# Row sums and gate totals added across partitions through memory instead of by mask matmuls

## The chip, the cores and the metric

The kernel runs on one core of one Trainium2 chip. The metric is the device time of one launch in microseconds (us). The core has these engines: PE (matrix products, with PEld for its weight loads), DVE, ACT and POOL (elementwise work on 128 partitions), and SP, whose instruction stream issues nearly all DMAs. Every engine works through its own stream in order; streams wait for each other by semaphores.

## The reference

q, k and v are [8 batches, 8 heads, 1152 tokens, 64] in float32. Queries are averaged in neighbouring pairs (576 left), then plain softmax attention per head:

```python
scores = scale * np.matmul(q_pool, k.transpose(0, 1, 3, 2))
attn = np.exp(scores - max); attn = attn / (np.sum(attn, axis=-1, keepdims=True) + 1e-09)
out = np.matmul(attn, v)
```

The heads are put side by side to x of [8, 576, 512]. Then, per batch, a mixture of depths: the score of a token is x times w_gate; the 128 tokens with the highest scores go through relu(xe @ w1) @ w2 (512 to 1024 to 512), and that, times sigmoid(score), is added to their rows of x; all other rows stay.

## The kernel before, in words

The unit of work is a **pair** of heads (32 pairs: 8 batches x 4), and each pair is done in two **halves** of 288 queries. A half goes through these steps, which `run` (L1210) issues for neighbouring halves in turn, so that all engine streams are fixed in the program's order:

- `scores` (L799): for each of 9 chunks of 128 keys, PE computes transposed scores (keys on partitions, queries of both heads along the row; four 64x64 tiles, L810), and ACT takes the exponential out of PSUM into p (L817). The maximum is not subtracted; a count at the end of the kernel falls back to another kernel if a sum was out of bounds.
- `folded` (L842): the sums over keys. POOL adds chunks to acc (L849, three instructions), DVE reduces p and acc through 32x32 transposes (L854) and adds the pieces (L863). What is left in the tile sum is, for each of four groups of 32 partitions, a partial sum: query i of a block stands on partition i of every group, and the four groups are still to be added.
- `weighted` (L819): PE multiplies p by v (L828), ACT copies the result out (L836), POOL adds its two parts (L838); `drained` turns it on DVE (L876), `multiplied` takes it times w_gate on POOL (L886).
- `normalized` (L893), once per pair: a matmul with the constant matrix merge (1 where two partitions have the same place in their group) adds the four groups and spreads the total to all partitions (L897); ACT adds 1e-9 and writes it into the tile sums (L907, two instructions); DVE takes the reciprocal rec (L914); POOL multiplies (x, L916). `stored` (L924) writes x to memory in the next second half.
- `gated` (L933): DVE reduces the products (L939) and multiplies by rec (L941): part, the share of this pair in the gate scores.
- `prepare_pair` (L719): POOL adds neighbouring queries (qp, L725), DVE turns keys and queries (kT, qT, L728 and L732) for the next pair, in the first half of a pair (the even one).

After a batch's fourth pair, `routed` (L957) is started. It is a generator, and `units` (L1204) advances it by one unit at the end of each half: out<-xs copies the batch (L964), line is the sum of part over pairs (L968); then a matmul with merge (L977) and an ACT copy (L981) make total, which goes to memory (L984) and comes back as a row on all partitions (L985) and as columns (L986, L987); two units of comparisons on DVE (L1031, L1040, L1050) and a third with the last comparisons and five picks (L1073: for each token tile, which of the 128 slots it takes); a unit with a matmul of the picks (L1083) and a gather by POOL (L1095); later the transposes (L1109), the first expert layer (L1120, 64 matmuls), and the second (L1133, 16 matmuls) with the scatter. So a batch's routing stretches over the halves of the next batches, and what stands next to what in PE's stream is set by the number of units.

`load_pair` (L697) issues on SP the loads of k, q and v of the pair after the next, at the start of a pair's second half. kb and qb have two buffers, v_sb three, and p two. A weight load follows in each of the first halves. The order on SP in a second half is: k, q, v of pair n + 2, the stores of x of pair n - 1, a weight piece.

## Time and profile before

| what | value |
|---|---|
| median of 3 runs (lowest to highest) | 734.17 us (733.55 to 735.32) |
| the profiled execution | 734.3 us |
| its span, first to last instruction | 732.6 us |
| DMA packets | 387,857, of them 375,648 under 512 B |
| L897, the mask matmul of a pair | 64 instructions, 290 ns each |
| L907, its two evictions on ACT | 64 instructions, 272 ns each |
| L914, the reciprocal | 32, 224 ns |
| DMAs k, q, v / x stores | 124 each of 144 KB / 128 of 72 KB |

A line of a group reads: line of the kernel, engine, operation, output<-input, shape and count, then busy us and mean ns of one, then idle time of the engine just before them and who ended it. A line of the timeline reads: start in us, duration in us, engine (SPq for DMAs issued by SP), line, operation, tiles, count, and in brackets the idle time before it and its releaser. A line of waits reads: who waited for whom, us in total, times, longest. Matmuls overlap their neighbours, so starts tell more than durations.

### The profile page before, as it was taken

To read this page: it belongs to the slowest core of one execution; us is meant where nothing else is said; L and a number is where in the kernel's file an instruction comes from. 1 tells how busy PE (TensorE), PEld (TensorE's weight loads), DVE (VectorE), ACT (ScalarE), POOL (GpSimd) and SP (SyncE) were. 2 spreads that over 40 slices of the span, in tenths; PEclk is the share of its full clock that TensorE was granted. 3 is DMA by queue.
4 is the path that set the end of the run, shared out by engine and by line. 5 is a ranking of instruction groups with operands and counts; after the bars stand their busy time and mean duration, and the time that the engine had idled before them with its cause. 6 is when DMAs were issued, how large, how long until landed. Compare 5 with 4: busy or idle time off the path is not lost. (4 is left out here: it accounts for less than half of the span.)

```text
span 732.6 us, 23508 instructions
## 1 busy us (share of the span) xinstructions
PE 719.4 (98%) x10096; PEld 493.4 (67%) x10096; DVE 519.6 (71%) x758; ACT 400.9 (55%) x772; POOL 480.6 (66%) x459
## 2 busy tenths in 40 slices
PE   8999999999999999999999999999999999999996
PEld 6678886768567685766757676576756768567663
DVE  3876668976499754997649885497856978479540
ACT  5666666564466634666446654666436664466320
POOL 5787777774676866757757666676657766577620
PEclk9999999999999999999999999999999999999998
DMA  8998897995487726967278562985628965351230
GB/s 164 175 180 168 171 194 131 144 150 130 85 146 129 129 82 107 152 101 130 82 140 141 98 110 87 156 138 106 100 87 156 145 106 110 78 103 18 37 103 22
DMA packets 387857, 87.67 MB, mean 120 GB/s; under 512 B 375648, under 2 KB 375648, under 8 KB 387488
## 3 DMA queue, kind: packets, MB, share of 16 engines
q1 hardware_dynamic: 386240, 81.30, 62.7%
q0 software_dynamic: 1280, 4.20, 2.0%
q8 instruction: 81, 1.33, 0.8%
q10 hardware_dynamic: 224, 0.59, 0.3%
q14 instruction: 32, 0.26, 0.1%
HBM read 74.50 MB, written 20.99 MB: 130 GB/s over the span
## 5 line engine op out<-in xcount | busy, mean ns | idle before, releaser
L817 ACT ACTIVATE p<-ps 128x576 f32<-128x576 f32 x576 | 319.5, 689 | 5.2 <-issue 3.5
L810 PE MATMUL ps<-qT,kT 64*64 64x288 f32 x4608 | 295.7, 406 | 0.5 <-DVE qT L794 0.5
L849 POOL TENSOR_TENSOR acc<-p 128x576 f32<-128x576 f32 x192 | 267.1, 1420 | 44.2 <-ACT p L817 42.4
L828 PE MATMUL ps<-p,v_sb 64*64 64x288 f32 x4608 | 293.9, 403 | 0.0
L828 PEld LDWEIGHTS ps<-p,v_sb 64*64 64x64 f32 x4608 | 204.1, 133 | 77.9 <-ACT p L817 15.2
L810 PEld LDWEIGHTS ps<-qT,kT 64*64 64x64 f32 x4608 | 177.6, 132 | 101.0 <-ACT p L817 27.3
L854 DVE TRANSPOSE_TENSOR_REDUCE fold<-p 128x54 f32<-128x1728 f32 x64 | 126.0, 1969 | 109.7 <-ACT p L817 109.7
L854 DVE TRANSPOSE_TENSOR_REDUCE fold<-acc 128x54 f32<-128x1728 f32 x64 | 124.9, 1951 | 57.0 <-POOL acc L849 57.0
L836 ACT COPY two<-ps 128x576 f32<-128x576 f32 x64 | 40.9, 640 | 206.4 <-PE ps L828 199.7
L916 POOL TENSOR_TENSOR x<-avb,rec 128x576 f32<-128x576 f32 x32 | 37.1, 1159 | 116.5 <-DVE rec L914 112.4
L838 POOL TENSOR_TENSOR av<-two 128x288 f32<-128x288 f32 x64 | 51.1, 798 | 18.4 <-ACT two L836 14.6
L1120 PEld LDWEIGHTS ps<-xeT,w 128*128 128x128 f32 x512 | 58.0, 192 | 3.7 <-issue 2.6
L1120 PE MATMUL ps<-xeT,w 128*128 128x128 f32 x512 | 59.7, 277 | 0.7 <-ACT xeT L1112 0.7
L1133 PE MATMUL ps<-w,hT 128*128 128x512 f32 x128 | 57.0, 597 | 0.0
L886 POOL TENSOR_TENSOR prod<-avb,w_gate 128x288 f32<-128x288 f32 x64 | 51.0, 797 | 1.9 <-DVE avb L876 1.9
L725 POOL TENSOR_TENSOR qp<-qb 128x576 f32<-128x576 f32 x31 | 43.5, 1403 | 7.3 <-DMA qb<-in_q_dram 7.3
L728 DVE STREAM_TRANSPOSE kT<-kb 128x1152 f32<-128x1152 f32 x31 | 42.4, 1369 | 0.3 <-issue 0.3
L1133 PEld LDWEIGHTS ps<-w,hT 128*128 128x128 f32 x128 | 23.6, 190 | 26.3 <-issue 26.3
L941 DVE TENSOR_TENSOR part<-red,rec 128x18 f32<-128x18 f32 x32 | 39.7, 1239 | 1.1
L1128 ACT ACTIVATE hT<-ps 128x512 f32<-128x512 f32 x16 | 9.6, 598 | 48.6 <-PE ps L1120 48.6
L1073 DVE TENSOR_SCALAR pick<-slot_f,rank 128x128 f32<-128x128 f32 (+1 forms) x40 | 32.8, 883 | 0.4
L876 DVE STREAM_TRANSPOSE avb<-av 128x288 f32<-128x288 f32 x64 | 29.1, 455 | 5.3 <-POOL av L838 5.2
(81 smaller groups left out, 313.2 us busy)
## 6 DMA issues: line engine op xcount, KB each, us to landing
kb<-in_k_dram SPq DMA_DIRECT2D x124, 144.0 KB, 4.3
qb<-in_q_dram SPq DMA_DIRECT2D x124, 144.0 KB, 4.6
v_sb<-in_v_dram SPq DMA_DIRECT2D x124, 144.0 KB, 4.0
xs<-x SPq DMA_DIRECT2D x128, 72.0 KB, 3.4
out_dram<-xs SPq DMA_DIRECT2D x8, 1152.0 KB, 5.8
w<-in_moe_w_dram SPq DMA_DIRECT2D x8, 512.0 KB, 5.0
sc_row<-row SPq DMA_DIRECT2D x7, 288.0 KB, 3.2
acc<-in_q_dram ACTq DMA_DIRECT2D x2, 288.0 KB, 5.3
```

Source lines behind the costliest of these rows:

```text
L725: nc.gpsimd.tensor_tensor(out=qp[:, :, :], in0=pair["q"][:, :, 0, :], in1=pair["q"][:, :, 1, :], op=ALU.add)
L728: nc.vector.transpose(kT.rearrange("p (c g i) -> p c g i", c=self.NC, i=BLK), pair["k"].rearrange("p (g c) d -> p c g d", c=self.NC),)
L810: nc.tensor.matmul(sc[keys, j, 0:n], lhsT=pair["kT"][rows, c * P + keys.start : c * P + keys.stop], rhs=pair["qT"][rows, qs], start=True, ...
L817: nc.scalar.activation(p[:, c // G, c % G, :, :], sc[:, :, 0:n], AF.Exp, scale=self.scale)
L828: nc.tensor.matmul(av[j * self.D : (j + 1) * self.D, e, 0:n], lhsT=half["pair"]["v"][keys, j, c, :], rhs=half["p"][keys, c // G, c % G, j, :],
L836: nc.scalar.copy(two[:, :, :], av[:, :, 0:n])
L838: nc.gpsimd.tensor_tensor(out=half["av"][:, :], in0=two[:, 0, :], in1=two[:, 1, :], op=ALU.add)
L849: nc.gpsimd.tensor_tensor(out=acc[:, u, :], in0=units[:, 0, u, :], in1=units[:, 1, u, :], op=ALU.add)
L854: nc.vector.tensor_reduce(fold[:, a, :], of.rearrange("p u (m d) -> p (u m) d", d=BLK), AX.X, ALU.add, apply_transpose=True,)
L886: self.nc.gpsimd.tensor_tensor(out=pair["prod"][:, ns, :], in0=pair["avb"][:, ns, :], in1=self.w_gate[:, hp : hp + 1, :].broadcast_to([P, ...
L1120: nc.tensor.matmul(pv[:, f, 0:w], lhsT=self.w1[:, c, (f0 + f) * P : (f0 + f + 1) * P], rhs=xeT[:, c, 0:w], start=(c == 0), stop=(c == self ...
L1133: nc.tensor.matmul(ps[0:w, 0 : self.Dm], lhsT=hT[:, f, 0:w], rhs=self.w2[:, f, :], start=(f == 0), stop=(f == self.NFC - 1),)
```

## The change

The row sums of a pair are no longer merged by a matmul. `sums_out` writes the tile sum (whose layout is now by head, then block) to memory, and `sums_back` reads it with four DMAs so that each lane gets the four partial sums of its query side by side in the tile five; a fifth place holds the constant 1e-9, and one DVE reduce adds the five. The last pair keeps the matmul and its two evictions. The totals of the gate go the same way for batches 0 to 5: part is written, read as 16 numbers per query, and reduced on DVE; the write and the read each have a unit of their own, so that `routed` yields once more there. Batches 6 and 7 keep the old way. `load_pair` is split: the loads of v (`load_values`) stand on SP between the write and the read of the sums.

```diff
--- before.py
+++ after.py
@@ -645,8 +645,12 @@
         nc.vector.tensor_copy(
             self.merge[:, :, :], self.same[:, :].unsqueeze(1).broadcast_to([P, P // BLK, BLK])
         )
-        self.tiny = const.tile([P, 1], F32, name="tiny")
-        nc.gpsimd.memset(self.tiny[:, :], 1e-9)
+
+        self.five = []
+        for i in range(2):
+            five = const.tile([P, 5, self.QB], F32, name=f"five{i}")
+            nc.gpsimd.memset(five[:, 4, :], 1e-9)
+            self.five.append(five)
     def tokens(self):
         nc = self.nc
@@ -696,25 +700,29 @@
     def load_pair(self, b, hp):
-
         nc = self.nc
         kb = self.load.tile([P, self.KB, BLK], F32, name="kb")
         qb = self.load.tile([P, self.QB, 2, BLK], F32, name="qb")
-        v_sb = self.load.tile([P, 2, self.NC, self.D], F32, name="v_sb", bufs=3)
         for j, ds, rows in self.quarters():
             of = self.k[b, 2 * hp + j, :, ds]
             nc.sync.dma_start(kb[rows, :, :], of.rearrange("(i n) d -> i n d", i=BLK))
         for j, ds, rows in self.quarters():
             of = self.q[b, 2 * hp + j, :, ds].rearrange("(i m) d -> i m d", i=BLK)
             nc.sync.dma_start(qb[rows, :, :, :].rearrange("i n r d -> i (n r) d"), of)
-        of = self.v[b, 2 * hp : 2 * hp + 2]
+        return {"k": kb, "q": qb, "b": b, "hp": hp}
+
+    def load_values(self, pair):
+
+
+        nc, hp = self.nc, pair["hp"]
+        v_sb = pair["v"] = self.load.tile([P, 2, self.NC, self.D], F32, name="v_sb", bufs=3)
+        of = self.v[pair["b"], 2 * hp : 2 * hp + 2]
         of = of.rearrange("j (i g c) d -> g i j c d", i=BLK, c=self.NC)
         for g in range(P // BLK):
             nc.sync.dma_start(
                 v_sb[g * BLK : (g + 1) * BLK, :, :, :].rearrange("i j c d -> i j (c d)"),
                 of[g].rearrange("i j c d -> i j (c d)"),
             )
-        return {"k": kb, "q": qb, "v": v_sb, "b": b, "hp": hp}
     def prepare_pair(self, pair):
@@ -859,13 +867,32 @@
                 apply_transpose=True,
             )
         if half["s"] == 0:
-            pair["sum"] = self.small.tile([P, 2, nb], F32, name="sum")
+            pair["sum"] = self.small.tile([P, 2, self.QB], F32, name="sum")
+        ns = slice(half["s"] * self.HB, (half["s"] + 1) * self.HB)
         nc.vector.tensor_reduce(
-            pair["sum"][:, half["s"], :],
-            fold.rearrange("p a (u n) -> p n (a u)", n=nb),
+            pair["sum"][:, :, ns],
+            fold.rearrange("p a (u j n) -> p j n (a u)", j=2, n=self.HB),
             AX.X,
             ALU.add,
         )
+
+    def last_pair(self, pair):
+        return pair["b"] == self.B - 1 and pair["hp"] == self.NPAIR - 1
+
+    def sums_out(self, pair):
+
+        row = pair["row"] = self.dram.tile([P, 2, self.QB], F32, name="row_sums")
+        self.nc.sync.dma_start(row[:, :, :], pair["sum"][:, :, :])
+
+    def sums_back(self, pair):
+
+        quad = P // BLK
+        five = pair["five"] = self.five[pair["hp"] % 2]
+        for j, _, rows in self.quarters():
+            self.nc.sync.dma_start(
+                five[rows, 0:quad, :],
+                pair["row"][:, j, :].rearrange("(g i) n -> i g n", i=BLK),
+            )
     def drained(self, half):
@@ -892,23 +919,28 @@
     def normalized(self, pair):
-        nc, hb, hp = self.nc, self.HB, pair["hp"]
-        ps = self.banks()[:, 0, :]
-        nc.tensor.matmul(
-            ps[:, 0 : 4 * hb],
-            lhsT=self.merge.rearrange("p g j -> p (g j)"),
-            rhs=pair["sum"].rearrange("p s n -> p (s n)"),
-            start=True,
-            stop=True,
-        )
+        nc, hp = self.nc, pair["hp"]
         tot = self.sums[:, pair["b"] * self.NPAIR + hp, :]
-        for j in range(2):
-            rows = slice(j * self.D, (j + 1) * self.D)
-            nc.scalar.activation(
-                tot[rows, :].rearrange("p (s n) -> p s n", s=2),
-                ps[rows, 0 : 4 * hb].rearrange("p (s j n) -> p s j n", s=2, j=2)[:, :, j, :],
-                AF.Identity,
-                bias=self.tiny[rows, 0:1],
+        if self.last_pair(pair):
+            ps = self.banks()[:, 0, :]
+            nc.tensor.matmul(
+                ps[:, 0 : 2 * self.QB],
+                lhsT=self.merge.rearrange("p g j -> p (g j)"),
+                rhs=pair["sum"].rearrange("p j n -> p (j n)"),
+                start=True,
+                stop=True,
+            )
+            for j in range(2):
+                rows = slice(j * self.D, (j + 1) * self.D)
+                nc.scalar.activation(
+                    tot[rows, :],
+                    ps[rows, j * self.QB : (j + 1) * self.QB],
+                    AF.Identity,
+                    bias=self.five[0][rows, 4, 0:1],
+                )
+        else:
+            nc.vector.tensor_reduce(
+                tot, pair["five"].rearrange("p g n -> p n g"), AX.X, ALU.add
             )
         rec = pair["rec"] = self.small.tile([P, self.QB], F32, name="rec")
         nc.vector.reciprocal(rec[:, :], tot)
@@ -964,21 +996,41 @@
         nc.sync.dma_start(self.out[b], xs[:, :])
-        line = self.small.tile([P, self.QB], F32, name="line")
-        nc.vector.tensor_reduce(
-            line[:, :], part[:, :, :].rearrange("p n q -> p q n"), AX.X, ALU.add
-        )
         sc = ffn.tile([P, NT], F32, name="gate_sc")
+        if b >= self.B - 2:
+            line = self.small.tile([P, self.QB], F32, name="line")
+            nc.vector.tensor_reduce(
+                line[:, :], part[:, :, :].rearrange("p n q -> p q n"), AX.X, ALU.add
+            )
         if b < self.B - 1:
-            yield True
+            total = self.small.tile([BLK, self.QB], F32, name="total")
+            if b < self.B - 2:
+                quad = P // BLK
+                row = self.dram.tile([P, self.NPAIR * self.QB], F32, name="row_gate")
+                nc.sync.dma_start(row[:, :], part.rearrange("p a n -> p (a n)"))
+                yield True
+                parts = self.small.tile([BLK, quad * self.NPAIR, self.QB], F32, name="parts", bufs=2)
+                nc.sync.dma_start(
+                    parts.rearrange("p (g a) n -> p g (a n)", g=quad),
+                    row.rearrange("(g i) x -> i g x", i=BLK),
+                )
+                yield True
+                nc.vector.tensor_reduce(
+                    total[:, :], parts.rearrange("p a n -> p n a"), AX.X, ALU.add
+                )
+            else:
+                yield True
+                ps = self.banks()[:, 0, 0 : self.QB]
+                nc.tensor.matmul(
+                    ps,
+                    lhsT=self.merge.rearrange("p g j -> p (g j)"),
+                    rhs=line[:, :],
+                    start=True,
+                    stop=True,
+                )
+                nc.scalar.copy(total[:, :], ps[0:BLK, :])
             sc_row = ffn.tile([P, NT * P], F32, name="sc_row")
-            ps = self.banks()[:, 0, 0 : self.QB]
-            nc.tensor.matmul(
-                ps, lhsT=self.merge.rearrange("p g j -> p (g j)"), rhs=line[:, :], start=True, stop=True
-            )
-            total = self.small.tile([BLK, self.QB], F32, name="total")
-            nc.scalar.copy(total[:, :], ps[0:BLK, :])
             row = self.dram.tile([Sp], F32, name="row")
             nc.gpsimd.memset(sc[:, NF:], 0.0)
             nc.sync.dma_start(row.rearrange("(i n) -> i n", i=BLK), total[:, :])
@@ -1219,6 +1271,8 @@
         self.prepare_first(upcoming)
         self.tokens()
         loaded = self.load_pair(*pairs[1]) if len(pairs) > 1 else None
+        if loaded:
+            self.load_values(loaded)
         weights = self.weight_loads()
         for h in range(n_halves + 1):
             if h < n_halves:
@@ -1241,6 +1295,13 @@
                 if h > 2:
                     self.gated(halves[h - 3])
                 self.folded(half)
+                if s == 1:
+                    if not self.last_pair(pair):
+                        self.sums_out(pair)
+                    if loaded:
+                        self.load_values(loaded)
+                    if not self.last_pair(pair):
+                        self.sums_back(pair)
                 if h > 1:
                     self.multiplied(halves[h - 2])
                 if s == 0 and loaded:
```

## The prediction

> **What bounds the kernel now.** I read the page's busy shares first, then the waits, then PE's timeline, and last DVE and POOL where PE meets them.
>
> ```profile
> PE 719.4 (98%) x10096; PEld 493.4 (67%) x10096; DVE 519.6 (71%) x758; ACT 400.9 (55%) x772; POOL 480.6 (66%) x459
> PEclk9999999999999999999999999999999999999998
> DMA  8998897995487726967278562985628965351230
> ```
>
> PE is busy for all but 13 us of the span at a full granted clock, so whatever leaves PE's stream shortens the run, until something makes PE wait. The DMA row is high in the first ten slices.
>
> ```profile
> L897 PE MATMUL ps<-sum,merge 128*128 128x36 f32 x64 | 13.2, 290 | 0.0
> L897 PEld LDWEIGHTS ps<-sum,merge 128*128 128x128 f32 x64 | 9.5, 188 | 14.0 <-issue 14.0
> ```
>
> These are the groups that leave PE. Their busy time is not their price, since matmuls overlap; the price is the step from start to start in PE's timeline:
>
> ```profile
> 314.93 4.59 PE L828 MATMUL ps<-p,v_sb 64*64 64x288 f32 x72
> 319.46 0.41 PE L897 MATMUL ps<-sum,merge 128*128 128x36 f32 x2
> 319.70 1.34 PE L1083 MATMUL ps<-meta,pick 128*128 128x3 f32 x10
> 320.98 4.60 PE L810 MATMUL ps<-qT,kT 64*64 64x288 f32 x72
> ```
>
> Here the mask matmul takes 0.24 us (319.46 to 319.70). The same stretch on DVE and POOL:
>
> ```profile
> 315.68 4.79 DVE L1073 TENSOR_SCALAR pick<-slot_f,rank 128x128 f32<-128x128 f32 x5
> 320.39 0.43 DVE L939 TENSOR_REDUCE red<-prod 128x9 f32<-128x288 f32 x1
> ...
> 313.94 4.14 POOL L849 TENSOR_TENSOR acc<-p 128x576 f32<-128x576 f32 x3 [1.34 <-ACT p L817]
> 318.03 0.80 POOL L886 TENSOR_TENSOR prod<-avb,w_gate 128x288 f32<-128x288 f32 x1
> 318.79 1.40 POOL L725 TENSOR_TENSOR qp<-qb 128x576 f32<-128x576 f32 x1
> ...
> PE ps L1083 <- DVE pick L1073: 0.6, 2, 0.3
> ```
>
> The five picks (selection masks that PE multiplies at L1083) take 4.79 us; the smallest of all picks takes 0.27. Cut finer, the timeline shows each ending as a POOL instruction ends (316.72, 318.08, 318.83, 320.19), so beside a POOL without gaps a pick lasts one POOL instruction. The last pick ends at 320.46; PE wants it about 1.0 us after L1083 starts, at 320.7. PE hardly waits for picks now (0.6 us in the run), with 0.3 us to spare.
>
> **The change on PE.** The profiled execution took 734.3 us (span 732.6 and 1.7 around it), 0.1 above the median of the runs, 734.17. Removed:
> - 31 of 32 L897: the matmul's step is 0.24 us, 7.4 in all.
> - 6 of 7 L977: 0.22 to 0.31 us of step, 1.4 in all.
> - Switches of tiling. L828 before an L897 steps 4.50 us on average, before L810 4.38; and L897 steps 0.34 instead of 0.24 when L810 follows: 0.22 per excursion into 128-row work. The order of instructions has 39 such excursions before and 27 after (expert work, moved by half a pair, now has odd halves of its own). 12 x 0.22 = 2.6.
> - ACT loses 62 evictions of 0.272 us that stood ahead of the exponentials; scores after an L897 step 4.42 against 4.37, with one of 4.80: about 1.0.
>
> Saving 12.4 us, taken as 12. Bounds: 9 (the two steps alone) and 15 (busy time of both groups).
>
> **What it adds beside PE.** DVE gets 31 reduces of 90 elements, between L968 (72 elements, 278 ns) and L863 (108, 340 ns): 0.3 us, 9.6 in all, hidden in DVE's idle 29% except in the chain below. Six reduces of 288 elements (L939 has 416 ns) replace six L968. L863's output order costs nothing: same count, an idle DVE. Each pair writes 128 pieces of 144 B and reads 512 of 72 B. The q1 queue took 62.7% of 16 x 732.6 us for 386,240 packets, 19 ns each, so 640 take 0.76 us of the 16 engines: hidden where the DMA share is 0.61 (170 to 690 us), not where it is 0.93 (first 100 us).
>
> SP issues 5 more DMAs per pair, 0.33 us (row<-total) to 0.43 us (gate_sc<-row): 1.8 us. The write waits for DVE's sum, and behind it on SP stand the next v, the reads and the next pair's k and q. From sum to total: 0.33 issue, 2.7 for four v issues (which cover the write's 1.8 us landing), 1.6 for four reads, 3.1 landing as gate_sc<-row: 7.7 us. In the trace 11.3 to 14.5 us lie between the end of a pair's second sum and its reciprocal from pair 6 on, so DVE does not wait there; it would begin to if landings took 3.6 us more. In pairs 0 to 5 the gap is only 8.0 to 11.8.
>
> **The chain to the picks, the term that decides.** The extra write and read of batches 0 to 5 push the routing units one half back. Comparisons start now in an odd half, right after the second expert layer (L1133), and the picks end the third half; PE wants them at the end of the fourth. After the change the comparisons again start right after that layer, but the three halves are even, odd, even. An even half has more on DVE: kT and qT (1.29 + 0.66 us of step), rec, total. Against before the chain grows by 2.1 + 0.15 + two totals 0.54 = 2.8 us. PE comes sooner by two L897 with their switches: 36.07 us from the anchor (start of the first scores after L1133, 283.63) becomes 35.25.
>
> Step by step from that anchor, with the trace's durations: fold(p) 5.86 (as now), first rec 12.7, four comparison blocks to 15.3, second fold done 20.8 (POOL's acc comes behind x, 14.3 to 18.5), two blocks to 24.0, part 24.9, third fold 29.1, kT, qT, avb, total, rec 31.85, last block 33.6. POOL then runs x to 33.15, acc to 37.6, prod to 38.4, av to 39.2 without a gap: the picks end at 34.9, 36.25, 37.65, 38.4 and 39.25. PE finishes L1083 at 39.5 instead of 36.5. PE waits **3.0 us per batch**; for batches 1 to 5, 15 us. Bounds: 0 (picks of 0.27 to 0.34 us from 33.6 end at 35.2), and 5.1, if part (L941), two inputs of 18 elements, waits through three POOL instructions for a gap (24.4 to 27.0): L941 has 0.18 to 4.63 us, so both occur. I take the boundary case, as in L941's 0.90. Batch 6 keeps the old unit and gets the fifth batch's expert layer inside its chain: no wait.
>
> [...]
>
> **The first 170 us.** SP issues there without a pause (7.7 to 103 us), some 18 us per pair, as PE's pace; POOL already waits for q once batch 0 routes:
>
> ```profile
> 112.27 3.50 SPq L706 DMA_DIRECT2D kb<-in_k_dram  x4
> 115.81 4.98 SPq L709 DMA_DIRECT2D qb<-in_q_dram  x4
> ...
> 124.41 1.41 POOL L725 TENSOR_TENSOR qp<-qb 128x576 f32<-128x576 f32 x1 [1.89 <-DMA qb<-in_q_dram]
> ```
>
> With 1.8 us of issues and 0 to 2 us of waiting for the write (behind k and q in the queue), SP falls 2 to 3 us per pair behind. Batch 0's write of part then lands only behind the 1.15 MB copy of xs (5.8 us), and SP waits for it. The issue of k at 112.27 moves to about 118.7, its q lands near 131 instead of 124.4, and the keys are turned by 133; PE wants them at 132.42 - 3 = 129.4. That is 3.6 us of PE wait, and batch 0's comparisons and picks, behind late totals, wait as the others or more. Together 8 us; bounds 0 (SP finds the queue drained and its issues shorter, as kb at 3.3 instead of 5.2 us) and 18 (batch 0's scores back only near 140 us, its picks 13 us late).
>
> **Sum:** 734.3 - 12 + 15 + 8 = 745.3; with the median's 0.1 less, 745.
>
> **Rivals.**
> 1. Faster: the picks find POOL's gaps. Then 734.3 - 12 + 0 to 8 = 722 to 730. For it: the smallest pick is 0.27 us, and POOL's ends are the only brake. Against it: POOL's own order is x, three accs, prod and av with nothing to wait for. It is decided by whether the last pick ends by 36.25 from the anchor; each us beyond costs 5.
> 2. SP becomes the bound through the early pairs and batch 0: the early term is 18, the picks 15 to 20: 755 to 760. For it: no SP pause up to 103 us and 0.93 DMA share. Against it: PE's second expert stages (7 us each) later let SP catch up.
> 3. The totals come late in every pair, landings 5 us above the row: 1.4 us of DVE wait per pair on margins of 3.6, doubled where two totals stand in the chain: 5 x 2.8 = 14 more, 759. Against it: in the steady part the DMA engines are 39% idle.
> 4. The matmuls go but their time does not, since the switches stay: saving 9 instead of 12, 748; inside the main case.
>
> **How the numbers follow.** Main case 0.54 (own range 737 to 754, from 2 to 5 us per batch and 2 to 12 early); rival 1 0.27; rivals 2 and 3 0.14; the pieces cancel to within 0.2% 0.05. 0.2% (1.5 us) is about what this measurement can tell from no change. Slower is 0.54 + 0.14 = 0.68, faster 0.27, same 0.05. The range reaches into rival 1 (723) and to the upper rivals' near edge (760); under 2 in 10 is left out.
>
> **What would show it.** PE: no L897 but one, one L977; stages after odd halves without expert work step 4.37 to 4.40. Right if the waits list PE (or its loads) at L1135 on DVE pick with 2 to 5 us each, six times. Rec on DVE should follow the second sum by 11 us or more after 190 us; in the first 150 us a wait of DVE on the five tile, and one of POOL on q. SP's waits should move from POOL's x to DVE's sum. Wrong if the waits at L1135 are under 1 us: then the picks are not chained to POOL's instructions in the new place. Wrong on the early term if k and q of pair 7 land by 126 us.

## The result, and the profile after

The changed kernel takes 774.85 us (median of four runs, 772.57 to 777.25) against 734.75 us (733.55 to 735.5) for the kernel before beside it: a ratio of 1.0548, interval 1.0509 to 1.0586, so 5.5% slower. The forecast was 745 us, range 723 to 760: the sign was right, the time lies outside the range. The profiled execution took 775.86 us (span 774.1); the one before 734.3 (span 732.6). The two spans differ by 41.5 us, and that is what has to be explained.

First the page of the changed kernel: the busy shares, the granted TensorE clock and the DMA row.

```profile
PE 727.4 (94%) x10022; PEld 504.3 (65%) x10022; DVE 513.6 (66%) x789; ACT 386.1 (50%) x704; POOL 479.8 (62%) x460
PEclk9999999869999999998999989999999999999998
DMA  8777886766564566645766546666466566551130
```

PE has 74 instructions fewer, and yet 8 us more of busy time: it works more slowly in places. The clock row, which was full before, has dips: a deep one at 155 to 175 us (6 tenths of full speed) and shallow ones (8 and 9 tenths) before and behind it. PE also waits now. From the list of waits (engine, waiting line, releaser: us in all, times, longest):

```profile
PE ps L1135 <- DVE pick L1125: 25.9, 31, 8.1
DVE sums L942 <- DMA five<-row_sums: 19.8, 5, 5.3
POOL qp L733 <- DMA qb<-in_q_dram: 7.0, 3, 3.6
PE ps L818 <- DVE qT L740: 5.6, 3, 2.5
```

The first line was 0.6 us before. L1135 multiplies the picks (it was L1083), L818 is the scores (it was L810). Here is the place in batch 2 that the forecast walked through step by step, as the timeline shows it on PE, DVE and POOL (start, us, engine, line):

```profile
347.88 4.69 PE L836 MATMUL ps<-p,v_sb 64*64 64x288 f32 x72
353.19 0.35 PE L1135 MATMUL ps<-meta,pick 128*128 128x3 f32 x2 [0.62 <-DVE pick L1125]
354.46 0.38 PE L1135 MATMUL ps<-meta,pick 128*128 128x3 f32 x2 [0.91 <-DVE pick L1125]
...
357.31 0.58 PE L1135 MATMUL ps<-meta,pick 64*128 64x3 f32 x2 [0.36 <-DVE pick L1125]
357.82 7.56 PE L818 MATMUL ps<-qT,kT 64*64 64x288 f32 x72
...
351.90 5.35 DVE L1125 TENSOR_SCALAR pick<-slot_f,rank 128x128 f32<-128x128 f32 x5
...
351.57 4.10 POOL L857 TENSOR_TENSOR acc<-p 128x576 f32<-128x576 f32 x3
355.64 0.79 POOL L913 TENSOR_TENSOR prod<-avb,w_gate 128x288 f32<-128x288 f32 x1
356.39 0.79 POOL L846 TENSOR_TENSOR av<-two 128x288 f32<-128x288 f32 x1
```

The picks run from 351.90 to 357.25 beside a POOL without gaps, PE takes them one by one, and the scores after them last 7.56 us instead of 4.6. The clock in that place, from the busy time by stretch (us, then busy time and instructions of PE, PEld, DVE, ACT, POOL, then the granted clock, the DMA share and GB/s):

```profile
317.00:358.00 41.00, 37.77 (x591) 27.93 (x594) 33.90 (x61) 23.09 (x44) 30.63 (x28) 0.99 0.58 103
358.00:363.00 5.00, 5.00 (x44) 2.59 (x47) 4.60 (x6) 2.79 (x7) 1.33 (x2) 0.50 0.23 59
363.00:373.00 10.00, 10.00 (x164) 5.82 (x160) 6.68 (x8) 6.04 (x11) 6.88 (x6) 0.96 0.75 139
```

In the 5 us after the wait the granted clock is 0.50. The kernel pays twice: for the wait, and for slow matmuls after it.

I then set the 63 points at which PE begins a half's scores in both traces side by side (halves are counted from 0, and the first two begin as one). The difference (after less before) reads:

| where | difference at that point | what happened since the row above |
|---|---|---|
| first scores | -1.0 | the start is earlier; a repeat of the kernel before was 0.4 earlier too |
| half 9 (87 us) | -3.6 | four pairs without L897: 0.64 us a pair saved |
| half 21 (213 us) | +20.7 | some 27 us lost (19.0 of waits and 8 of slow work, lines below), so about 3 saved meanwhile |
| half 63 (676 us) | +41.5 | batches 1 to 5: waits 20.9 and slow scores 9.7; 9.9 saved, which is what is left over |

A half with picks lasts 14.09 to 14.31 us from scores to scores in batches 1 to 5, against 10.06 without a wait (8.78 of a half and 1.28 of the picks' matmuls in the trace before): 4.0 to 4.25 us of wait each, 20.9 in five batches. The scores' step after it is 5.82, 7.39, 6.50, 6.10 and 5.93 us against 4.41: 1.4 to 3.0 us each, 9.7 in all.

The early loss, as PE's timeline of the changed kernel shows it:

```profile
113.40 6.28 PE L818 MATMUL ps<-qT,kT 64*64 64x288 f32 x72 [2.00 <-DVE qT L740]
135.35 6.17 PE L818 MATMUL ps<-qT,kT 64*64 64x288 f32 x72 [2.53 <-DVE qT L740]
151.32 4.34 PE L818 MATMUL ps<-qT,kT 64*64 64x288 f32 x40 [3.50 <-ACT p L825]
168.17 0.56 PE L1135 MATMUL ps<-meta,pick 128*128 128x3 f32 x2 [8.09 <-DVE pick L1125]
172.80 6.22 PE L818 MATMUL ps<-qT,kT 64*64 64x288 f32 x72
```

PE waits 5.6 us for qT (1.09 of it earlier, at 93.67 us), 3.5 us for exponentials (p) and 9.9 us for batch 0's picks (8.09 and four shorter waits), 19.0 in all. The slow scores with and after these waits and the drawn-out picks make up the other 8.

### The profile page after: what moved, and what is told of

It reads as the page before. It is cut to its first block, busy times and chain, and to the rows that moved or that the text cites. A ratio compares the mean times of both kernels' runs of the same rounds, so it can differ in the third digit from the quotient of the medians.

```text
span 774.1 us, 23555 instructions
## 1 busy us (share of the span) xinstructions
PE 727.4 (94%) x10022; PEld 504.3 (65%) x10022; DVE 513.6 (66%) x789; ACT 386.1 (50%) x704; POOL 479.8 (62%) x460
## 3 DMA queue, kind: packets, MB, share of 16 engines
q8 instruction: 81, 1.33, 0.7%
## 5 line engine op out<-in xcount | busy, mean ns | idle before, releaser
L818 PE MATMUL ps<-qT,kT 64*64 64x288 f32 x4608 | 309.9, 420 | 9.8 <-DVE qT L740 5.6
L818 PEld LDWEIGHTS ps<-qT,kT 64*64 64x64 f32 x4608 | 192.8, 138 | 112.9 <-issue 23.9
L1135 PE MATMUL ps<-meta,pick 128*128 128x3 f32 (+1 forms) x80 | 16.2, 284 | 25.9 <-DVE pick L1125 25.9
L1125 DVE TENSOR_SCALAR pick<-slot_f,rank 128x128 f32<-128x128 f32 (+1 forms) x40 | 36.8, 983 | 0.4
L1135 PEld LDWEIGHTS ps<-meta,pick 128*128 128x128 f32 (+1 forms) x80 | 13.6, 220 | 32.1 <-DVE pick L1125 16.5
```

Of the source, the lines that this page charges most:

```text
L818: nc.tensor.matmul(sc[keys, j, 0:n], lhsT=pair["kT"][rows, c * P + keys.start : c * P + keys.stop], rhs=pair["qT"][rows, qs], start=True, ...
```

## The experiments

Before them stood theory A: three costs, the early transfers behind SP's queue, the picks one half later, and a lower clock after each wait of PE. Theory B: only the gate's totals cost anything, the row sums through memory are nearly free. Theory C: the traffic through memory as such.

Where a ratio is given, it is against the kernel before on the same chip. That kernel took medians of 735 to 741 us on the chips used, so differences of a few us between runs of different groups are read from the traces and not from the medians.

### The two halves of the change, and where they begin

Row sums alone (gate totals of all batches by the matmul):

```diff
-        if b >= self.B - 2:
+        if not (False):
             line = self.small.tile([P, self.QB], F32, name="line")
...
-            if b < self.B - 2:
+            if False:
                 quad = P // BLK
```

> The row sums go through memory as in the change, the gate's totals of all batches stay with the mask matmul, so nothing of the gate's routing is a half later. Theory A (three costs: the early lag of SP, the picks one half later in batches 1 to 5 at 4.2 us each, and 1.4 to 3 us each in which TensorE runs at a lower granted clock after such a wait): the five waits at L1135 are gone with what follows them (some 30 us), and part of the early loss of 28 us, so 728 to 738 us. Theory B (the row sums through memory cost nothing, the gate's totals are the whole loss): 720 to 724 us, the time before less a saving of 11 to 15 us. Theory C (the traffic through memory slows everything): above 745 us.

Measured: 744.9 us, ratio 1.012 (1.0086 to 1.0155).

The gate's totals alone (row sums of all pairs by the matmul, v loaded where it was before):

```diff
     def last_pair(self, pair):
-        return pair["b"] == self.B - 1 and pair["hp"] == self.NPAIR - 1
+        return True
...
                     loaded = self.load_pair(*pairs[n + 2]) if n + 2 < len(pairs) else None
+                    if loaded:
+                        self.load_values(loaded)
```

> The mirror image: row sums by the mask matmul and the loads of v at their old place, the gate's totals of six batches through memory with their extra half. Theory A: five waits of 4.2 us, each followed by a slow stretch of 1.4 to 3 us, and the routing of batch 0 late, without the lag of the row sums on SP: 753 to 760 us, and the mean wait of L1135 on the pick again above 4 us. Theory B: the whole loss is here, with only the gate's small part of the saving: 760 to 775 us. Theory C: six writes and 24 reads in all are little, so 740 us or less.

Measured: 763.76 us, ratio 1.0385 (1.035 to 1.042).

Both from batch 2 on:

```diff
     def last_pair(self, pair):
-        return pair["b"] == self.B - 1 and pair["hp"] == self.NPAIR - 1
+        return pair["b"] < 2 or (pair["b"] == self.B - 1 and pair["hp"] == self.NPAIR - 1)
...
-            if b < self.B - 2:
+            if 2 <= b < self.B - 2:
```

> Both routes through memory begin with batch 2; batches 0 and 1 stay with the mask matmul for row sums and gate totals. Theory A: the early loss of 28 us is gone, as are the wait and the slow stretch of batch 1 (6 us), and the saving of the eight pairs too (4 us): about 750 us. The rival, that the early loss has nothing to do with the transfers but with the order of v's loads, which is unchanged here: 765 us or more.

Measured: 748.48 us, ratio 1.0173 (1.0144 to 1.0202), as theory A had it.

Neither part is free: 9.7 us over the kernel before for the row sums, 28.6 for the gate's totals, 38.3 together, close to the 40.1 of the whole change. So B falls, and A had both too cheap (728 to 738 and 753 to 760 us). With the row sums alone the difference to before goes from -3.4 us at half 9 to +18.3 at half 16, and then falls to +10.4 at the end. That is a loss of some 22 us within seven halves and 7.9 us of gain after it. With the gate's totals alone it is +7.3 at half 17, and then it rises with each batch to +29.6. With both from batch 2 on it stays at -1.0 until half 18, falls to -5.1 by half 31, and rises from half 32 on, with batch 2's picks. C falls too: it had the gate's totals at 740 us or less, and if the traffic as such were slow, the row sums, which are most of it, would lose throughout, and they gain after half 16.

### Why the picks hold PE up

The picks in a form that also sums into a column that nobody uses:

```diff
                     scalar1=rank[0:rows, t : t + 1],
                     scalar2=None,
                     op0=ALU.is_equal,
+                    op1=ALU.add,
+                    accum_out=hits[0:rows, t : t + 1],
```

> The change as it is, but each pick (a comparison by VectorE) also sums into a column, a form that in this kernel's trace does not stand behind POOL. If the picks are late because each one lasts as long as the POOL instruction beside it (5.35 us for the run of them), they now end some 3 us or more earlier and the waits of L1135 on the pick shrink from 4.2 us to 1 us or less: about 750 us by theory A (4 to 5 us less in each of five batches, and less in batch 0). The rival, that the picks are late because their scores come back late and their own length does not matter: 770 to 775 us.

Measured: 744.87 us, ratio 1.0112 (1.0078 to 1.0145), 30 us less than the change with its own picks. The same place of batch 2 on DVE, PE and POOL:

```profile
346.65 0.34 DVE L1126 TENSOR_SCALAR_CACHE_REDUCE pick<-slot_f,rank 128x128 f32<-128x128 f32 x1
346.92 0.08 DVE L1126 DVE_READ_ACCUMULATOR pick<-slot_f,rank 128x1 f32 x1
...
347.25 1.36 PE L1138 MATMUL ps<-meta,pick 128*128 128x3 f32 x10
348.55 4.60 PE L818 MATMUL ps<-qT,kT 64*64 64x288 f32 x72
...
346.31 4.13 POOL L857 TENSOR_TENSOR acc<-p 128x576 f32<-128x576 f32 x3
```

A pick now takes 0.34 us where five took 5.35, 1.07 each on average; PE does not wait, and the scores after take 4.60. POOL is as busy as before beside it. So the start of the picks, as late as in the change (8.4 us after the start of the half's scores in both), does no harm by itself; the length of the picks beside POOL does.

The gate's write and read in one unit, with the copy of the batch's output behind them:

```diff
-        nc.sync.dma_start(self.out[b], xs[:, :])
...
                 nc.sync.dma_start(row[:, :], part.rearrange("p a n -> p (a n)"))
-                yield True
...
                 )
+                nc.sync.dma_start(self.out[b], xs[:, :])
                 yield True
```

> The change with one difference: the gate's partial sums are written and read back in one unit, ahead of the copy of the batch's output, so the extra unit is gone and the totals are added where the matmul stood before. If the loss in batches 1 to 5 comes from the extra unit (every later step of the routing one half later, so that the picks meet POOL and TensorE waits for them), the waits of L1135 on the pick shrink to 1 us or less and the time is 744 to 752 us, as with the faster picks. The rival, that the two trips through memory alone make the picks late, the unit or not: 768 to 775 us.

Measured: 748.52 us, ratio 1.0112 (1.0082 to 1.0143) on a chip where the kernel before took 740.66. In batches 1 to 4 PE does not wait for picks by more than 0.1 us, in batch 5 by 0.62 us. So the extra unit and the slow picks are both needed for the cost in batches 1 to 5: taking away either removes it. The early loss is in both runs (+20.9 us at half 21 with the accumulating picks, +17.0 with one unit).

### The lower clock after a wait

The kernel before, with seven needless reductions on DVE ahead of the picks of batches 0 to 5:

```diff
             pick = ffn.tile([P, NT, P], F32, name="pick", bufs=1)
+            if b < self.B - 2:
+                idle = ffn.tile([P, 1], F32, name="idle", bufs=1)
+                for _ in range(7):
+                    nc.vector.tensor_reduce(
+                        idle[:, :], self.slot_f[:, :], AX.X, ALU.max
+                    )
```

> The kernel before, nothing through memory; only seven needless reductions on VectorE (some 4.5 us) stand ahead of the picks of batches 0 to 5. It asks whether a wait of TensorE alone is followed by a lower granted clock. If it is: six waits of some 4 us and after each 1.4 to 3 us in slower matmuls, 33 to 42 us in all, so 766 to 777 us, with a granted clock below 0.7 in the 5 us after each wait. If the lower clock belongs to the traffic through memory: the waits alone, some 24 us, so 756 to 760 us, at a clock that stays near 1.00.

Measured: 758.6 us, ratio 1.0257 (1.0225 to 1.0288). By its time alone this would be the second answer, but the waits came out shorter than I had made them: 1.51 us in each of batches 1 to 5. The trace answers instead: first PE's timeline in batch 1, then the busy time and clock of the stretches around it:

```profile
235.66 0.41 PE L897 MATMUL ps<-sum,merge 128*128 128x36 f32 x2
237.58 1.37 PE L1089 MATMUL ps<-meta,pick 128*128 128x3 f32 x10 [1.51 <-DVE pick L1079]
238.89 6.19 PE L810 MATMUL ps<-qT,kT 64*64 64x288 f32 x72
```

```profile
230.00:235.00 5.00, 5.00 (x85) 2.92 (x84) 4.86 (x13) 2.71 (x5) 4.86 (x4) 1.00 0.96 144
235.00:240.00 5.00, 3.48 (x37) 2.40 (x32) 4.90 (x11) 1.30 (x5) 2.18 (x3) 0.87 0.84 166
240.00:245.00 5.00, 5.00 (x72) 2.80 (x68) 4.97 (x6) 4.19 (x8) 0.00 (x0) 0.78 0.01 3
```

With no partial sums going through memory, a wait of 1.5 us is followed by scores at a clock of 0.78. Their step is 6.02 to 6.11 us against 4.41, four times of five 6.10 or more: another 1.6 to 1.7 us. Of the 21.8 us by which this span is longer than before, each of batches 1 to 5 takes about 3.3, half of it wait and half clock. The lower clock belongs to the pause in PE's work, not to the trips of partial sums. How its cost goes with the pause, over the runs (idle time listed at the picks' matmul, then the scores' step, 4.41 without a pause):

| run | idle us | step us |
|---|---|---|
| row sums alone, batch 5 | 0.62 | 4.42 |
| one unit, batch 5 | 0.62 | 6.11 |
| kernel before once more, batch 0 | 1.33 | 4.42 |
| kernel before with delay, batches 1 to 5 | 1.51 | 6.02 to 6.11 |
| gate alone, batches 1 to 5 | 1.46 to 1.50 | 6.00 to 7.35 |
| the change, batches 1 to 5 | 2.83 to 3.24 | 5.82 to 7.39 |
| row sums alone, batch 0 | 8.81 | 6.82 |

The cost hardly follows the length. At 0.62 us it came once and stayed out once, at 1.33 us it stayed out, and from 1.5 us on it is 1.4 to 3.0 us whatever the length. The clock's own record shows what it goes with. In all 17 traces the granted clock is either 1.00 or 0.50, and it changes only on a grid of 3.41 us: a low stretch before the end of the kernel lasts 3.41, 6.83, 10.24 or 13.65 us, and each 3.41 us at half clock costs up to 1.7 us (half of its length, an estimate; after the waits of 1.51 us it was 1.6 to 1.7 us). Here are the two pauses of 0.62 us on that grid, first the run with one unit, then the one with the row sums alone:

```profile
598.17:601.58 3.41, 2.79 (x34) 2.08 (x34) 3.38 (x6) 1.13 (x4) 1.70 (x2) 1.00 0.64 97
601.58:604.99 3.41, 3.41 (x36) 1.93 (x32) 3.38 (x4) 2.62 (x5) 0.00 (x0) 0.50 0.84 132
```

```profile
594.49:597.90 3.41, 3.15 (x47) 1.93 (x38) 3.41 (x5) 0.64 (x1) 3.23 (x4) 1.00 0.50 117
597.90:601.31 3.41, 3.05 (x46) 2.14 (x49) 3.38 (x5) 1.71 (x5) 0.65 (x1) 1.00 0.75 116
601.31:604.72 3.41, 3.41 (x64) 2.17 (x60) 3.38 (x4) 3.41 (x7) 0.00 (x0) 1.00 0.90 142
```

In the first run the picks' matmuls and the pauses between them all fall into one window, which keeps 1.34 us of other matmuls, and the clock is 0.50 in the next; in the second they lie across a border, each window keeps 2.3 us or more, and the clock stays at 1.00. Cut into such windows, all 17 traces sort without an exception: where PE, in a window at full clock, was busy with anything but the picks' matmuls for at most 1.42 us, the clock was 0.50 in the next (56 windows); where for 1.49 us or more, it stayed at 1.00 (3528 windows). With the picks' matmuls counted as work no limit sorts them (2.80 us was followed by half clock, 1.49 us by full). So these thin matmuls, three columns each, count like pause here, and what a pause costs depends on how it lies on the grid. No run was made to move a pause along it; the sorting is read from the traces.

### The first 170 us

Row sums through memory for all pairs but the 4th, gate by the matmul:

```diff
     def last_pair(self, pair):
-        return pair["b"] == self.B - 1 and pair["hp"] == self.NPAIR - 1
+        return (pair["b"] == 0 and pair["hp"] == 3) or (
+            pair["b"] == self.B - 1 and pair["hp"] == self.NPAIR - 1
+        )
```

> Row sums through memory for every pair but the 4th, the last of batch 0; gate totals by the mask matmul, picks as they were. If the whole early loss of 22 us follows from that one pair (its sum is the last thing that batch 0's gate total waits for, and all of its routing comes after): 724 to 731 us. If the trips of pairs 5 to 8 are late on their own account: 737 to 745 us, hardly better than all pairs through memory (744.9 us).

Measured: 745.41 us, ratio 1.0079 (1.0052 to 1.0106), no better than with all pairs (744.9). With all pairs, PE stood 6.55 us ahead of batch 0's gate total (at 109.34 us) and 8.81 ahead of its picks. Here the first of these waits is gone, but PE only comes sooner to the next one, for the queries of the 8th pair:

```profile
135.48 6.07 PE L818 MATMUL ps<-qT,kT 64*64 64x288 f32 x72 [5.45 <-DVE qT L740]
141.37 4.55 PE L836 MATMUL ps<-p,v_sb 64*64 64x288 f32 x72
152.73 1.24 PE L1135 MATMUL ps<-meta,pick 128*128 128x3 f32 x4 [6.81 <-DVE pick L1125]
```

So it is not one late total; something shared is late. Two runs with row sums from batch 2 on and all gate totals by the matmul separate what. The first is without any early trip:

```diff
     def last_pair(self, pair):
-        return pair["b"] == self.B - 1 and pair["hp"] == self.NPAIR - 1
+        return pair["b"] < 2 or (pair["b"] == self.B - 1 and pair["hp"] == self.NPAIR - 1)
...
-            if b < self.B - 2:
+            if False:
```

> Row sums through memory from batch 2 on only, all gate totals by the mask matmul. In the run with all row sums through memory the kernel lost 22 us between the 9th and the 16th half and then gained 7.9 us over the rest. If the loss belongs to the first 150 us, when the DMA engines are most loaded and no expert layer lies between the halves, this run keeps the gain and about 1 us at the start: 725 to 728 us, faster than before. The rival, that the loss comes wherever the transfers begin or meets the routing of any batch: 735 us or more.

Measured: 729.64 us, ratio 0.9869 (0.9842 to 0.9895). No early loss, though v stands at its new place in SP's queue, and half a us where the trips begin. The second makes the early trips and lets nobody read what they bring:

```diff
-                    if not self.last_pair(pair):
+                    if not self.real_last(pair):
                         self.sums_out(pair)
...
-                    if not self.last_pair(pair):
+                    if not self.real_last(pair):
                         self.sums_back(pair)
```

(`last_pair`, which chooses the matmul, is true for batches 0 and 1; `real_last` for the last pair alone.)

> Row sums of batches 0 and 1 are added by the mask matmul, as in the run with row sums from batch 2 on (729.6 us), but their trips through memory are made all the same: written, waited for by SP's queue and read back into a tile that nobody reads in these pairs. If SP's queue is what made the first 170 us late: the loads of the 8th pair are issued some 8 us later, TensorE waits for its q and then for the picks, and 10 to 20 us are lost: 740 to 750 us. If the waits of VectorE and POOL for the totals are the cause, the trips alone cost next to nothing: 729 to 733 us.

Measured: 740.09 us, ratio 1.0054 (1.003 to 1.0078). In the traces the unread trips cost 10.5 us, all between halves 13 and 15: PE waits 7.61 us for the 8th pair's qT, and the scores after it take 7.08 us instead of 4.6. SP's queue in that stretch, first without the trips:

```profile
103.45 0.59 SPq L996 DMA_DIRECT2D out_dram<-xs  x1
105.53 0.33 SPq L1036 DMA_DIRECT2D row<-total  x1
111.20 0.35 SPq L1037 DMA_DIRECT2D sc_row<-row  x1
...
112.76 3.52 SPq L708 DMA_DIRECT2D kb<-in_k_dram  x4
```

and with them:

```profile
110.47 0.42 SPq L890 DMA_DIRECT2D row_sums<-sum  x1
...
114.98 3.07 SPq L897 DMA_DIRECT2D five<-row_sums  x4
118.09 0.59 SPq L1001 DMA_DIRECT2D out_dram<-xs  x1
118.77 0.52 SPq L1041 DMA_DIRECT2D row<-total  x1
124.31 0.35 SPq L1042 DMA_DIRECT2D sc_row<-row  x1
...
125.80 3.82 SPq L710 DMA_DIRECT2D kb<-in_k_dram  x4
```

The same k of the 8th pair is issued 13.0 us later, though nobody waits for a row sum in these pairs: behind write, v, reads, output and the scores' row in one queue. The lag builds up pair by pair. When SP issues the write, counted from the end of the pair's second sum on DVE, and how long after the write the first read is issued:

| pair | unread trips: write after sum | the change: write after sum | the change: read after write |
|---|---|---|---|
| 1 | 0.1 | 1.1 | 4.3 |
| 2 | 4.5 | 4.6 | 4.4 |
| 3 | 8.4 | 4.6 | 4.3 |
| 4 | 9.7 | 3.6 | 4.2 |
| 5 | 11.8 | 2.7 | 5.7 |
| 6 | 16.8 | 8.2 | 2.6 |
| 8 | 2.9 | 0.03 | 2.3 |
| 11 | 0.03 | 0.04 | 2.3 |

SP is the bound of the first six pairs. In the change the lag stays smaller; DVE waits for the totals there (19.8 us in five waits), which would hold the rest back together with SP. From the 8th pair on SP is there as the sum ends (0.03 to 0.04 us after it in the change), and none of DVE's five waits for totals lies there (the last ends at 141 us): the trip costs nothing. The row sums alone lose 22 us there and the unread trips 10.5; that the rest, some 11 us, is the wait of DVE and then of POOL and PE for totals that come late out of the same queue is what the waits in the trace name, and was not separated by a run.

### What is left when both costs are taken out

The picks' new form on the kernel before, in two groups of runs:

```diff
                     op0=ALU.is_equal,
+                    op1=ALU.add,
+                    accum_out=hits[0:rows, t : t + 1],
```

> The kernel before with the picks in the form that also sums into a column. It asks whether the length of the picks was on the path before the change. By the trace of before TensorE waited 0.6 us in all for picks, so 733 to 735 us (no difference). If picks held up the end of a half in a way the waits do not name: 731 us or less.

Measured: 733.86 us, ratio 0.9912 (0.9882 to 0.9941): the time as expected, but not the "no difference".

> The kernel before with the faster picks, a second time, since in its first comparison the kernel before itself ran 6 us longer than on the chips of the other comparisons. If the form of the picks is no gain by itself: 733 to 735 us and a ratio of 0.997 to 1.002. If it is one: a ratio of 0.994 or less again.

Measured: 734.22 us, ratio 0.9933 (0.9907 to 0.9959). The kernel before took 740.66 and 739.87 us beside them, against 734 to 735 in the first comparisons. To see why, its profile was taken once more beside another group:

> The kernel before, unchanged, for a profile beside the others of this group. If it is the picks that hold it up where it takes 738 to 742 us: TensorE waits for picks in each batch by 0.6 us or more, and the matmuls after the wait are at a lower granted clock. If the chip is slower throughout: no new wait, and every half is longer.

Measured: 736.36 us, ratio 1.0004 (0.998 to 1.0029). The profiled execution was a quick one (span 733.3): PE waits 1.3 us for the picks of batch 0 and for none after, and all else is as in the first profile. So the picks of batch 0 are on the edge of PE's path before the change; whether the executions of 738 to 743 us have a longer pause there with its slow clock was not seen in a profile. The mean clock on record with each execution leans that way: on the chip of the 739.87 us it is 0.997 or 0.998 in those of up to 738.3 us and 0.993 to 0.996 in those of 740 us and more, and one stretch of 3.41 us at half clock takes 0.0023 off such a mean (estimate). The form of the picks is worth 0.7 to 0.9% on the two chips where it was run; on that of the first comparisons, where the kernel before takes 734 to 735 us, it was not.

Three versions of the change with that form follow. The first sends the row sums of all pairs but the 4th to 8th through memory, and no gate totals:

```diff
     def last_pair(self, pair):
-        return pair["b"] == self.B - 1 and pair["hp"] == self.NPAIR - 1
+        return (
+            (pair["b"] == 0 and pair["hp"] == 3)
+            or pair["b"] == 1
+            or (pair["b"] == self.B - 1 and pair["hp"] == self.NPAIR - 1)
+        )
...
-            if b < self.B - 2:
+            if False:
```

> Row sums through memory for all pairs but the 4th to the 8th (the pairs whose sums fed the waits of the first 170 us), gate totals by the mask matmul, picks in the faster form. By the theory that the early loss sits in these five pairs alone: the time with row sums from batch 2 on (729.6 us) less 1.5 to 2.5 us for the first three pairs and up to 1 us for waits on picks, so 726 to 728 us and about 1% under before. The rival, that any early pair through memory makes the routing of batch 0 late: 735 us or more.

Measured: 729.76 us, ratio 0.9868 (0.9836 to 0.9899).

The second differs from it in the gate's totals of batches 2 to 5, which go through memory:

```diff
-            if False:
+            if 2 <= b < self.B - 2:
```

> As the kernel before this one in the list, with the gate's totals of batches 2 to 5 through memory as in the change, in their later half. If with the faster picks the extra half costs nothing, four matmuls with their copies fall away, some 0.4 us each: 724 to 727 us. The rival, that the extra half still costs its share: 730 us or more.

Measured: 730.56 us, ratio 0.9869 (0.9839 to 0.9899).

The third sends row sums through memory from batch 2 on, and no gate totals:

```diff
     def last_pair(self, pair):
-        return pair["b"] == self.B - 1 and pair["hp"] == self.NPAIR - 1
+        return pair["b"] < 2 or (pair["b"] == self.B - 1 and pair["hp"] == self.NPAIR - 1)
...
                     op0=ALU.is_equal,
+                    op1=ALU.add,
+                    accum_out=hits[0:rows, t : t + 1],
```

> Row sums through memory from batch 2 on, gate totals by the mask matmul, and the faster picks. If the picks still hold TensorE up a little where it runs ahead (1.0 us in three waits in the run without them): 727 to 729 us. If not: the same 729.6 us as without.

Measured: 723.66 us (723.39 to 723.8 in six runs), ratio 0.9826 (0.9798 to 0.9853): the fastest, and 10 us under the kernel before with the same picks. My expectation of 727 to 729 was too high: besides the picks of batch 0, this run keeps small gains in the later batches that the run with the old picks does not (-10.4 us at half 63 against -5.3), and I have not traced these further. The first two missed their 726 to 728 us and 724 to 727 us. In the first, PE comes 2.7 us sooner through the first three pairs (0.7 of it at the start), and then stands 2.1 us for a pair's sum, 2.3 for q and 2.0 for picks, at a mean granted clock of 0.997 in the profiled execution against 0.999 in the third. What is saved in the first 80 us is lost again in these three places; that the loads set the pace there is my reading, not shown by a run of its own. The gate's totals through memory gain nothing that can be measured there, even where PE does not wait for the picks. Of the third, two lines of the page and one of the waits:

```profile
PE 710.5 (98%) x10050; PEld 480.5 (67%) x10050; DVE 505.8 (70%) x821; ACT 387.8 (54%) x726; POOL 480.3 (67%) x460
PEclk9999999999999999999999999999999999999999
```

```profile
PE ps L1138 <- DVE pick L1126: 0.3, 1, 0.3
```

PE is busy for 98% again, at a full clock, on fewer instructions than before; it no longer waits for picks beyond 0.3 us. That is the change's idea, kept to where a trip through memory is free.

## Why the prediction was wrong

- **The saving was 12 us; it is about 17** (1.0 at the start, 2.6 in four pairs, about 3 until half 21, and 9.9 after, the last as what is left over). That is over the upper bound of 15, the busy time of the removed groups, though up to 0.4 of the start is spread between executions. The row sums alone give 0.64 us a pair in the first four, where the price of 0.24 for the matmul's step and 0.22 per switch had said less. The error helped.
- **The chain to the picks was right in its steps and its place.** From the anchor, the start of the first scores after the second expert layer, rec was to come at 31.85 and came at 32.5 (349.78 after 317.27); the picks were to begin at 33.6 and end at 39.25, and they began at 34.6 and ended at 39.98. The wait was taken as 3.0 us a batch and measured 4.0 to 4.25, 20.9 in five instead of 15, inside the bounds of 0 to 5.1. That the picks' length beside POOL decides, and not the late chain alone, is shown by the run with the other form.
- **Left out: the clock after a wait.** This step failed outright: the sum priced a wait of PE at its length and the slow work after it at nothing. The scores after each wait take 1.4 to 3.0 us more, 9.7 in five batches, and again after the early waits. The trace before has no long pause in its steady part, and its clock row is full, so no row there showed it; a bound upwards was missing. The run with a delay shows that it comes without the new trips.
- **The first 170 us: 8 us taken, bounds 0 to 18, about 27 measured.** This is the largest error, and the term that failed is not the one that was worked out step by step. For q of the 8th pair 3.6 us of PE's wait were priced; k was issued at 122.2 us and q landed at 133.0, against 118.7 and 131, and PE waited 2.53 us. (The sign of being wrong, a landing by 126 us, did not appear; the error lay on the other side.) What failed is the rest of the term, some 4.4 us for batch 0's comparisons and picks "as the others or more": PE stood 9.9 us ahead of those picks, and besides 3.1 us for qT of two earlier pairs, 3.5 us for exponentials, and some 8 us in slow scores and drawn-out picks, all of which the sum had at nothing. The lag of 2 to 3 us a pair was near: with nobody waiting for the totals SP falls 1.3 to 5.0 us per pair behind, 16.8 us by the 6th pair; but the working let it add up to 6.4 us at the 8th pair's k, where the unread trips alone made it 13.0. The wait of DVE for the totals, named for pairs 1 to 6, was seen (five times, 5.3 us at most). What made batch 0's picks so late, beyond the queue, stays open in part: the unread trips account for 10.5 us of the 22 that the row sums lose.
- **Rival 2** (SP the bound of the early pairs, early 18, picks 15 to 20, 755 to 760) was nearest in mechanism, with 18 us for the early part still too low; it lacked the clock. With 9.7 us after the five waits, 21 for the waits and 27 early, less 17, the sum is 734.3 - 17 + 21 + 9.7 + 27 = 775, which only puts the measured parts together again. I gave it, with rival 3, 0.14: its evidence, a queue of SP without a pause, had been read and then discounted, on the ground that SP's later slack lets it catch up. It does catch up, but after the damage.
- **Rival 1** (the picks find POOL's gaps) did not happen. **Rival 3** (totals late in every pair) did not either: from the 8th pair on the first read is issued 2.3 us after the write and DVE does not wait; its totals come some 10 to 18 us after the sums, where I had said 11 or more. **Rival 4** (the saving stays at 9) is excluded.
- **The range** had 760 as its end. It held one bad case at a time; the early term and the picks being bad together, with a cost after each wait, was not in it. The main case's own range, 737 to 754, is also narrower than its stated ends: 2 to 5 us for each of five batches and 2 to 12 early give 734 to 759.

My own later reading failed as well: theory A put the row sums alone at 728 to 738 us and they took 744.9, the gate's totals alone at 753 to 760 and they took 763.76, and in a second try I laid the whole early loss on the 4th pair.

## What to carry to other kernels

A transfer that waits for another transfer, put into a queue that also loads the next stage, is not priced by its issue time (here the trips that nobody read moved the 8th pair's k by 13.0 us, where the working had 6.4): ask how late the queue already is at that place, and let the lag add up stage by stage until the queue has slack. Where the main engine runs without a pause at a full clock, price any new wait at its length plus the slow work after it, in this case up to 1.7 us (estimate) for each stretch of 3.41 us at half clock; here a wait of 1.5 us cost 3.3, and after one of 1.33 us that lay otherwise on the grid the scores were not slow. And before moving a chain by half a stage, look at what its last instructions will stand beside: here one form of the same comparison took three times as long as another beside a busy POOL (1.07 us on average against 0.34), and changing that form recovered 30 us of the 40 lost.

## What was not expected of the hardware

- A pause of 1.5 us on TensorE was followed by a granted clock of 0.78 over the next 5 us (0.50 after the longer pauses of the change), and by 1.4 to 3.0 us more in the next scores: 1.6 to 2.9 us after 1.5 us of pause, 2.4 us after 8.8. In the 17 traces the clock went with windows of 3.41 us: after one with at most 1.42 us of work other than the picks' thin matmuls it was halved (56 windows), after one with 1.49 us or more it was not (3528).
- A comparison of 128x128 elements that also accumulates took 0.34 us beside a POOL at work, and five that do not took 5.35 us together.
- In the first five pairs, with digits 7 and 8 in the page's DMA row, the read was issued 4.2 to 5.7 us after the write of 18 KB that it waits for; later 2.3 us after it, and there the write and the four loads of v between them take that long to issue (0.33 and 1.79 us at 246 us), so that nothing was left to wait for.
